# Fused cross-covariance attention and MLP on one core: scores of batch 0 transposed into two PSUM banks, a small first chunk, and v block 2 loaded behind the weights

## The chip, the cores and the metric

One core of one Trainium2 chip runs the whole program. The metric is device time in microseconds (us), lower is better. Most executions of the kernel before agree within 0.3%.

## The reference, cut to what matters

```python
# q, k, v: (4, 6080, 256); moe_w_in: (256, 2048); moe_w_out: (2048, 256)
qn = q / (norm(q, axis=1) + 1e-6);  kn = k / (norm(k, axis=1) + 1e-6)
a  = softmax(kn.transpose(0, 2, 1) @ qn / tau)      # 256 x 256 per batch
x  = (v @ a).reshape(24320, 256)
out = gelu_tanh(x @ w_in) @ w_out
```

Each batch needs all of its q and k before a 256 x 256 matrix is known; then 6080 rows of v stream through it. The kernel folds `a @ w_in` into one matrix `aw` per batch, so that a block of 512 rows costs `hp = v @ aw`, a gelu, and `yp = g @ w_out`.

## The kernel before: the parts that matter here

Batch 0 has nothing to hide behind. Its q and k are loaded in chunks; each is cast (VectorE, DVE), squared (ScalarE, ACT) and multiplied into G (TensorE, PE):

```python
    first_chunks = chunks_of([12, 12, 5, 6, 4, 4, 2, 2], 2)   # slots of 128 rows
    TAIL, SHARED = 4, 6
    fillers = [0, 0, 5, 7, 4, 3, 1, 0]        # idle matmuls that keep the clock up
    ...
    for n, ch in enumerate(first_chunks):
        ...                                    # cast, square
        keep_clock(fillers[n])
        ...                                    # G += k^T q;  cols += column sums of the squares
```

The weights follow the q and k in the load queue. GpSimd (POOL) casts them and, between the casts, issues the loads of v blocks 1 and 2:

```python
    for half in range(2):
        ...                                    # w_in: two loads, two casts
        load_v(1 + half)
    for half in range(2):
        w = flat_stage(8)
        nc.sync.dma_start(out=w, in_=wout_v[:, half * 8 : half * 8 + 8, :])
        nc.gpsimd.tensor_copy(wout_bf[:, half * 8 : half * 8 + 8, :], w)
```

Then the serial end of the head: root of the column sums, scaling of G, four transposes into one tile T, two exponentials, the first columns of `aw`, and the first hp:

```python
    T = turned(Gs)                             # four transposes into one PSUM tile
    keep_clock(1, pY, "y")
    ...
    for jc in range(2):
        nc.scalar.activation(eT[:, jc, :], T[:, jc, :], AF.Exp, scale=r[:, jc : jc + 1])
```

v itself has to be turned. Block 0 and block 1 are turned by TensorE, all later blocks by DMA transposes, which SyncE (SP) issues at the start of the block two before:

```python
        for blk in range(n_blocks):
            vT = vT_of.pop(nb)
            turn_v(nb + 2)                     # four DMA transposes of v block nb + 2
            load_v(nb + 3)                     # GpSimd's queue
            for i in range(NP):                # hp, gelu, and yp of the block before
```

GpSimd's queue also carries batch 1's q and k, from step 3 of block 0 on.

Of the kernel before, what the change touches and what calls it, by code (L numbers as in the profile page):

```python
# [8 lines left out]
FP32 = mybir.dt.float32  # L9
BF16 = mybir.dt.bfloat16  # L10
AF = mybir.ActivationFunctionType
# [7 lines left out]
def kernel(  # L19
# [10 lines left out]
    nc = tc.nc  # L30
# [29 lines left out]
    pA = ctx.enter_context(tc.tile_pool(name="pA", bufs=2, space=bass.MemoryType.PSUM))  # L60
    pH = ctx.enter_context(tc.tile_pool(name="pH", bufs=2, space=bass.MemoryType.PSUM))
    pY = ctx.enter_context(tc.tile_pool(name="pY", bufs=2, space=bass.MemoryType.PSUM))
# [7 lines left out]
    def chunks_of(sizes, with_rem):  # L70
        found, s0 = [], 0
        for n, size in enumerate(sizes):
            found.append((s0, size, n == with_rem))
            s0 += size
        assert s0 == S_ALL
        return found
# [12 lines left out]
    def slots_of(chunk, rest=REM):  # L89
        _, size, rem = chunk  # L90
        return [(s, 128) for s in range(size)] + ([(size, rest)] if rem else [])
# [1 line left out]
    n_all = S_ALL + 1  # L93


    first_chunks = chunks_of([12, 12, 5, 6, 4, 4, 2, 2], 2)
    TAIL, SHARED = 4, 6
    fillers = [0, 0, 5, 7, 4, 3, 1, 0]
    staged = []

    def halves(pool, tag, dtype, size, most=SMAX):

        tiles = [pool.tile([128, 2, most, 256], dtype, tag=tag, name=tag)
                 for _ in range(1 if size <= most else 2)]
        if len(tiles) == 1:
            return [tiles[0][:, x] for x in range(2)], tiles[0]
        return [t.rearrange("p a b c -> p (a b) c") for t in tiles], None
# [21 lines left out]
    ident = const.tile([128, 128], FP32)  # L129
# [20 lines left out]
    def keep_clock(n, pool=pH, tag="h"):  # L150

        for _ in range(n):
            idle = pool.tile([128, 2, 512] if pool is pH else [128, 512], FP32, tag=tag, name="idle")
            nc.tensor.matmul(idle[:, 0, :] if pool is pH else idle, lhsT=filler[:, 0:128], rhs=filler, start=True, stop=True)
# [37 lines left out]
    def turned(Gs):  # L192
        T = pA.tile([128, 2, 256], FP32, tag="a", name="T")
        for ic in range(2):
            for jc in range(2):
                nc.tensor.matmul(T[:, jc, ic * 128 : ic * 128 + 128],  # L196
                                 lhsT=Gs[:, ic, jc * 128 : jc * 128 + 128],
                                 rhs=ident, is_transpose=True)
        return T

    def row_sums(eT):
        rs = pA.tile([128, 512], FP32, tag="a", name="rs")
        for ic in range(2):
            for jc in range(2):
                nc.tensor.matmul(
                    rs[:, ic : ic + 1],
                    lhsT=eT[:, jc, ic * 128 : ic * 128 + 128],
                    rhs=ones_bf,
                    start=jc == 0, stop=jc == 1)
        rsinv = smx.tile([128, 2], FP32, tag="rsinv", name="rsinv")  # L210
        nc.vector.reciprocal(rsinv, rs[:, 0:2])
        return rsinv
# [19 lines left out]
    n_chunks = len(first_chunks)  # L232
    seen, summed = 0, 0

    def sums_of(parts, last):
        nonlocal summed
        for m, x in enumerate(parts):
            col_sums(cols, x, ones_bf[: x[0].shape[0], :], summed == 0, last and m == len(parts) - 1)
            summed += 1
# [16 lines left out]
    for n, ch in enumerate(first_chunks):  # L256
        st, whole = staged[n]
        size = ch[1]
        qkb, qk_whole = halves(qkp, "qk", BF16, size)
        sqb, sq_whole = halves(sqp, "sq", BF16, size)  # L260
        hi = size + ch[2]
        if whole is None:
            todo = list(zip(qkb, sqb, st))
        else:
            todo = [[y[:, :, 0:hi] for y in (qk_whole, sq_whole, whole)]]
        for to, sq, x in todo:
            nc.vector.tensor_copy(to, x)  # L267
            if n != n_chunks - 2:
                nc.scalar.activation(sq, x, AF.Square)  # L269
        if n == n_chunks - 2:  # L270
            nc.scalar.activation(sqb[1][:, 0:hi], st[1][:, 0:hi], AF.Square)
            nc.vector.tensor_mul(sqb[0][:, 0:hi], qkb[0][:, 0:hi], qkb[0][:, 0:hi])
        keep_clock(fillers[n])
        for s, rows in slots_of(ch, 128):
            gram(G, qkb, s, rows, seen == 0, seen == n_all - 1)
            seen += 1
        if waiting is not None:
            pairs_of(*waiting)
            waiting = None
        if n < 2:  # L280
            pairs_of(n, sqb)
        elif n < TAIL:
            waiting = (n, sqb)
        else:
            sums_of([[y[:rows, s, :] for y in sqb] for s, rows in slots_of(ch, 128)], n == n_chunks - 1)

        for x in ((2, 3) if n == 0 else (4, 5) if n == 1 else (n + 4,)):
            stage_chunk(x)

    v0 = stage.tile([128, 2, SMAX, 256], FP32, tag="st", name="v0")  # L290
# [11 lines left out]
    def load_v(nb):  # L302
        if nb >= B * n_blocks:
            return
        r0, n, rest = v_parts(nb)
        t = vin.tile([128, 4, 256], BF16, tag="v", name="vb")
        nc.gpsimd.dma_start(  # L307
            out=t[:, 0:n, :],
            in_=v_rows[r0 : r0 + n * 128, :].rearrange("(p s) c -> p s c", s=n))
        if rest:  # L310
            nc.gpsimd.dma_start(out=t[:rest, n, :], in_=v_rows[r0 + n * 128 : r0 + n * 128 + rest, :])
        v_of[nb] = t
# [36 lines left out]
    for half in range(2):  # L349
        w = flat_stage(2)  # L350
        for x in range(2):
            c0 = half * 1024 + x * 512
            nc.sync.dma_start(out=w[:, :, x * 512 : x * 512 + 512], in_=win_v[:, :, c0 : c0 + 512])
            nc.gpsimd.tensor_copy(win_bf[:, :, c0 : c0 + 512], w[:, :, x * 512 : x * 512 + 512])
        load_v(1 + half)
    for half in range(2):
        w = flat_stage(8)
        nc.sync.dma_start(out=w, in_=wout_v[:, half * 8 : half * 8 + 8, :])
        nc.gpsimd.tensor_copy(wout_bf[:, half * 8 : half * 8 + 8, :], w)  # L359


    r = smx.tile([128, 4], FP32, tag="r", name="r")
# [3 lines left out]
    Gs = scaled(G, r)  # L366
    vps = []
    for cc in range(2):
        p = pH.tile([128, 2, 512], FP32, tag="h", name="vps")[:, 0, :]
        for s in range(4):  # L370
            nc.tensor.matmul(p[:, s * 128 : s * 128 + 128],
                             lhsT=v0[:, s, cc * 128 : cc * 128 + 128],
                             rhs=ident, is_transpose=True)
        vps.append(p)
    keep_clock(1, pY, "y")
    T = turned(Gs)
    keep_clock(1, pY, "y")
    vT0 = vts.tile([128, 2, 512], BF16, tag="vT", name="vT")
    nc.vector.tensor_copy(vT0[:, 0, :], vps[0])
    eT = smx.tile([128, 2, 256], BF16, tag="eT", name="eT")  # L380
    aw = awp.tile([128, 2, D], BF16, tag="aw", name="aw")
    for jc in range(2):
        nc.scalar.activation(eT[:, jc, :], T[:, jc, :], AF.Exp, scale=r[:, jc : jc + 1])  # L383
    nc.scalar.activation(vT0[:, 1, :], vps[1], AF.Copy)


    firsts = []

    def first_aw(n, jc, pool=pY, tag="y"):

        if jc == 0:
            firsts.append(pool.tile([128, 512], FP32, tag=tag, name="ps"))
        nc.tensor.matmul(
            firsts[n][:, 0:256],
            lhsT=eT[:, jc, n % 2 * 128 : n % 2 * 128 + 128],
            rhs=win_bf[:, jc, n // 2 * 256 : n // 2 * 256 + 256],
            start=jc == 0, stop=jc == 1)

    first_aw(0, 0)
    first_aw(1, 0)  # L400
    rsinv = row_sums(eT)
    first_aw(0, 1)
    first_aw(1, 1)
    for n in (2, 3):
        first_aw(n, 0, pA, "a")
        first_aw(n, 1)
    for n in range(4):
        ic, lo = n % 2, n // 2 * 256
        dst, scale = aw[:, ic, lo : lo + 256], rsinv[:, ic : ic + 1]
# [2 lines left out]
        else:  # L412
            nc.vector.tensor_scalar_mul(dst, firsts[n][:, 0:256], scale)  # L413
    nc.scalar.activation(dummy, ones_f, AF.Gelu_apprx_tanh)
    aw_left = [(fs, ic, *((pA, "a") if fs == 2 else (pY, "y"))) for fs in range(1, 4) for ic in range(2)]

    def more_aw(n):
        for _ in range(n):
# [18 lines left out]
    def attention_steps(b, aw_next):  # L437
# [50 lines left out]
        yield  # L488
        T = turned(Gs)
        eT = smx.tile([128, 2, 256], BF16, tag="eT", name="eT")  # L490
        if abs(inv_tau) > TANH_MAX:
            for jc in range(2):
                nc.scalar.activation(eT[:, jc, :], T[:, jc, :], AF.Exp, scale=r[:, jc : jc + 1])
            yield
# [67 lines left out]
    for b in range(B):  # L562
# [5 lines left out]
        for blk in range(n_blocks):  # L568
# [27 lines left out]
            for i in range(NP):  # L596
                at_slot.update(g=g, i=i)
                hp = pH.tile([128, 2, 512], FP32, tag="h", name="hp")
                for j in range(2):
                    fc = 2 * i + j  # L600
                    for cc in range(2):
                        nc.tensor.matmul(hp[:, j, :cols],  # L602
                                         lhsT=aw[:, cc, fc * 128 : fc * 128 + 128],
                                         rhs=vT[:, cc, :cols],
# [4 lines left out]
                if before is not None:  # L609
                    n = -(-len(before["todo"]) // (NP - i))  # L610
                elif i >= NP - 3:

                    n = 4
                else:
                    n = 0
# [14 lines left out]
    for c0 in (0, 128):  # L630
        yp = pY.tile([128, 512], FP32, tag="y", name="yp")[:, 0:128]
        for fc in range(FC):
            nc.tensor.matmul(yp, lhsT=before["g"][:, fc, s * 128 : s * 128 + 128],  # L633
                             rhs=wout_bf[:, fc, c0 : c0 + 128], start=fc == 0, stop=fc == FC - 1)
# [39 lines left out]
```

## Time and profile before

| | value |
|---|---|
| median of 6 runs | 753.86 us (753.45 to 754.20) |
| last k chunk of batch 0 landed | 34.28 us |
| first hp matmul | 40.06 us |
| waits of PE after that | one over 0.25 us: yp on w_out, 0.71 us |
| span of the profiled run | 752.0 us |

The profile is read in three pieces. Up to 34 us loading sets the pace; from there to 40 us a chain of small steps; after 40 us PE, without a gap worth naming. In that last piece any idle microsecond of PE is one of the total. The lines are in the prediction.

### The profile page before, as it was taken

How to read it: one execution, taken by the hardware profiler on the slowest of the kernel's cores; microseconds unless marked ns; L12 is line 12 of the kernel's file. 1: busy time of each engine (PE TensorE's matmuls, PEld its weight loads, DVE VectorE, ACT ScalarE, POOL GpSimd, SP SyncE). 2: the span in 40 equal slices, each digit the busy share in tenths (PEclk: the TensorE clock that was granted, in tenths of full speed). 3: DMA queues.
4: the chain of work that ended last, by engine and by line, in shares of the span. 5: the costliest groups of instructions: out<-in, count | busy, mean ns of one | idle time of the engine just before them, and what ended most of it. 6: DMA issues, size and time to landing. Idle time of an engine off the chain costs nothing.

```text
span 752.0 us, 12341 instructions
## 1 busy us (share of the span) xinstructions
PE 726.4 (97%) x5186; PEld 502.3 (67%) x5274; DVE 284.3 (38%) x497; ACT 420.3 (56%) x411; POOL 80.8 (11%) x154
## 2 busy tenths in 40 slices
PE   2899999999999999999999999999999999999998
PEld 1656766776666766776666666776666666666666
DVE  3733556463501646554521265555351011011011
ACT  4875555556456555555555555555645655555552
POOL 1061111101012102101001102010101000000000
PEclk9999999999999999999999999999999999999999
DMA  9989685613237685824325876671413533322111
GB/s 369 400 205 200 104 150 139 132 43 69 70 72 144 114 163 108 164 63 75 71 57 117 141 119 124 150 143 46 69 43 85 105 85 70 69 75 54 41 57 57
DMA packets 80183, 85.69 MB, mean 114 GB/s; under 512 B 55424, under 2 KB 59136, under 8 KB 79616
## 3 DMA queue, kind: packets, MB, share of 16 engines
q0 software_dynamic: 14480, 30.87, 25.7%
q1 hardware_dynamic: 65344, 52.39, 24.4%
q10 hardware_dynamic: 304, 1.64, 0.5%
q8 instruction: 41, 0.67, 0.4%
q14 instruction: 14, 0.11, 0.0%
HBM read 78.91 MB, written 24.90 MB: 138 GB/s over the span
## 4 chain that ended last, share of the span: by engine, by line
PE 94%; DMA 3%; ACT 1%; issue 1%; DVE 0%; POOL 0%; SPq 0%; DVEq 0%; POOLq 0%
PE yp L528 44%; PE hp L602 43%; PE G L158 4%; PE ps L218 2%; ACT sq L269 1%; DMA st<-in_q_dram 1%; DMA st<-in_k_dram 1%; PE T L196 0%; POOL wout_bf L359 0%; PE yp L633 0%; PE cols L170 0%; DVE qk L267 0%; DVE aw L413 0%; DVE Gs L188 0%; ACT eT L383 0%
## 5 line engine op out<-in xcount | busy, mean ns | idle before, releaser
L606 ACT ACTIVATE g<-hp 128x1024 bf16<-128x1024 f32 (+1 forms) x384 | 389.8, 1015 | 307.0 <-PE hp L602 295.2
L528 PE MATMUL yp<-wout_bf,g 128*128 128x256 bf16 x3024 | 392.0, 273 | 1.6 <-POOL wout_bf L359 0.7
L602 PE MATMUL hp<-vT,aw 128*128 128x512 bf16 (+1 forms) x1456 | 383.9, 377 | 3.8 <-DVE aw L413 0.2
L528 PEld LDWEIGHTS <-g 128*128 128x128 bf16 x3024 | 295.9, 98 | 114.3 <-issue 1.2
L602 PEld LDWEIGHTS <-aw 128*128 128x128 bf16 x1536 | 149.9, 98 | 104.1 <-DVE aw L413 0.5
L545 DVE COPY ysb<-yp 128x512 f32<-128x512 f32 (+1 forms) x95 | 64.9, 683 | 396.5 <-PE yp L528 396.5
L460 DVE TENSOR_TENSOR acc<-acc,sq 128x512 f32<-128x512 f32 x141 | 97.6, 692 | 4.8
L459 DVE TENSOR_TENSOR sq<-qkb 128x512 bf16<-128x512 bf16 x141 | 58.9, 418 | 0.0
L158 PE MATMUL G<-qkb 128*128 128x256 bf16 x288 | 55.0, 273 | 0.0
L307 POOL DMA_DIRECT2D vb<-in_v_dram x47 | 25.9, 552 | 88.6 <-DMA vT<-vb 81.3
L227 DVE TENSOR_SCALAR aw<-ps,rsinv 128x512 bf16<-128x512 f32 x30 | 22.4, 749 | 23.5 <-PE ps L218 18.3
L158 PEld LDWEIGHTS <-qkb 128*128 128x128 bf16 x288 | 28.2, 98 | 3.3
L332 POOL CAST gate<-g 1x1 f32<-1x1 bf16 x24 | 5.9, 245 | 227.8 <-ACT g L606 227.8
L158 PE MATMUL G<-qk 128*128 128x256 bf16 x96 | 13.5, 298 | 15.8 <-DVE qk L267 15.8
L269 ACT ACTIVATE sq<-st 128x3072 bf16<-128x3072 f32 (+2 forms) x9 | 21.1, 2379 | 11.1 <-DMA st<-in_q_dram 8.2
L158 PEld LDWEIGHTS <-qk 128*128 128x128 bf16 x96 | 9.8, 106 | 19.1 <-DVE qk L267 16.6
L267 DVE CAST qk<-st 128x3072 bf16<-128x3072 f32 (+2 forms) x10 | 14.2, 1438 | 13.1 <-DMA st<-in_q_dram 10.0
L218 PE MATMUL ps<-win_bf,eT 128*128 128x512 bf16 x54 | 16.4, 379 | 0.2
L479 POOL TENSOR_TENSOR r<-r,half 128x4 f32<-128x4 f32 x3 | 3.1, 1042 | 103.4 <-DVE r L478 103.4
L82 POOL DMA_DIRECT2D qkb<-in_q_dram x24 | 12.9, 537 | 5.8 <-issue 4.3
L585 POOL COPY g<-gr 128x1024 bf16<-128x1024 bf16 x2 | 2.1, 1036 | 101.3 <-PE yp L528 101.3
L82 POOL DMA_DIRECT2D qkb<-in_k_dram x24 | 12.9, 539 | 0.0
(73 smaller groups left out, 109.0 us busy)
## 6 DMA issues: line engine op xcount, KB each, us to landing
out_dram<-ysb SPq DMA_DIRECT2D x44, 512.0 KB, 3.0
vb<-in_v_dram POOLq DMA_DIRECT2D x43, 256.0 KB, 6.2
qkb<-in_q_dram POOLq DMA_DIRECT2D x21, 384.0 KB, 4.6
qkb<-in_k_dram POOLq DMA_DIRECT2D x21, 384.0 KB, 6.4
st<-in_q_dram SPq DMA_DIRECT2D x2, 1536.0 KB, 11.8
vT<-vb SPq DMA_TRANSPOSE x184, 3.0
wst<-in_moe_w_in_dram SPq DMA_DIRECT2D x4, 512.0 KB, 7.5
wst<-in_moe_w_out_dram SPq DMA_DIRECT2D x2, 1024.0 KB, 11.7
```

The costliest lines, as they stand in the source:

```text
L82: engines[x].dma_start(out=dst[x][:, 0:size, :], in_=src[b, s0 * 128 : (s0 + size) * 128, :].rearrange("(p s) c -> p s c", s=size))
L158: nc.tensor.matmul(G[:, ic, :], lhsT=qk[1][:rows, s, ic * 128 : ic * 128 + 128], rhs=qk[0][:rows, s, :], start=first and ic == 0, stop=las ...
L218: nc.tensor.matmul(ps, lhsT=eT[:, jc, ic * 128 : ic * 128 + 128], rhs=win_bf[:, jc, fs * 512 : fs * 512 + 512], start=jc == 0, stop=jc == 1)
L227: nc.vector.tensor_scalar_mul(dst, ps, scale)
L269: nc.scalar.activation(sq, x, AF.Square)
L307: nc.gpsimd.dma_start(out=t[:, 0:n, :], in_=v_rows[r0 : r0 + n * 128, :].rearrange("(p s) c -> p s c", s=n))
L459: nc.vector.tensor_mul(sq[:rows], flat, flat)
L460: nc.vector.tensor_add(acc[:rows], acc[:rows], sq[:rows])
L528: nc.tensor.matmul(yp[:rows, at, :], lhsT=g[:, fc, s * 128 : s * 128 + rows], rhs=wout_bf[:, fc, :], start=fc == 0, stop=fc == FC - 1)
L545: nc.vector.tensor_copy(ysb[:, s0 : s + 1, :], yp[:, 0 : s + 1 - s0, :])
L602: nc.tensor.matmul(hp[:, j, :cols], lhsT=aw[:, cc, fc * 128 : fc * 128 + 128], rhs=vT[:, cc, :cols], start=cc == 0, stop=cc == 1)
L606: nc.scalar.activation(g[:, 2 * i : 2 * i + 2, :cols], hp[:, :, :cols], AF.Gelu_apprx_tanh)
```

## The change

Its intent: let the first exponential start before all four transposes are done, begin work on a small first chunk, and take v block 2's load out of the way of w_out, for which yp waited.

```diff
-    first_chunks = chunks_of([12, 12, 5, 6, 4, 4, 2, 2], 2)
-    TAIL, SHARED = 4, 6
-    fillers = [0, 0, 5, 7, 4, 3, 1, 0]
+    first_chunks = chunks_of([2, 12, 12, 5, 6, 4, 2, 2, 2], 3)
+    TAIL, SHARED = 4, 7
+    fillers = [0, 0, 0, 5, 7, 4, 1, 1, 0]
 ...
-        load_v(1 + half)
+        if half == 0:
+            load_v(1)
     for half in range(2):
         w = flat_stage(8)
 ...
+    load_v(2)
 ...
-    T = turned(Gs)
-    keep_clock(1, pY, "y")
+    T = [pY.tile([128, 512], FP32, tag="y", name="T") for _ in range(2)]
+    for ic in range(2):
+        for jc in range(2):
+            nc.tensor.matmul(T[jc][:, ic * 128 : ic * 128 + 128], ...)   # cut
 ...
-        nc.scalar.activation(eT[:, jc, :], T[:, jc, :], AF.Exp, scale=r[:, jc : jc + 1])
+        nc.scalar.activation(eT[:, jc, :], T[jc][:, 0:256], AF.Exp, scale=r[:, jc : jc + 1])
```

Cut: the staging of the chunks that goes with the new sizes (the squares of two chunks before the last, where it was one, are split between ACT and DVE), and the PSUM pools of the first products, which swap places, with the row sums moved to a third pool. `TAIL` stays 4, but with one chunk more in front it now leaves the chunk of six among those whose squares are summed slot by slot, 24 column-sum matmuls where pairs took 12.

More of the change, by code (lines that the diff above doesn't have):

```diff
@@ L199, in turned, with row_sums @@
         return T
-    def row_sums(eT):
-        rs = pA.tile([128, 512], FP32, tag="a", name="rs")
+    def row_sums(eT, rs=None):
+        if rs is None:
+            rs = pA.tile([128, 512], FP32, tag="a", name="rs")
         for ic in range(2):
@@ L267 @@
             nc.vector.tensor_copy(to, x)
-            if n != n_chunks - 2:
+            if n not in (n_chunks - 3, n_chunks - 2):
                 nc.scalar.activation(sq, x, AF.Square)
-        if n == n_chunks - 2:
+        if n in (n_chunks - 3, n_chunks - 2):
             nc.scalar.activation(sqb[1][:, 0:hi], st[1][:, 0:hi], AF.Square)
@@ L279 @@
             waiting = None
-        if n < 2:
+        if n < 3:
             pairs_of(n, sqb)
@@ L285 @@
             sums_of([[y[:rows, s, :] for y in sqb] for s, rows in slots_of(ch, 128)], n == n_chunks - 1)
-        for x in ((2, 3) if n == 0 else (4, 5) if n == 1 else (n + 4,)):
+        for x in ((2,) if n == 0 else (3, 4) if n == 1 else (5, 6) if n == 2 else (n + 4,)):
             stage_chunk(x)
@@ L375 @@
     keep_clock(1, pY, "y")
-    T = turned(Gs)
-    keep_clock(1, pY, "y")
+    T = [pY.tile([128, 512], FP32, tag="y", name="T") for _ in range(2)]
+    for ic in range(2):
+        for jc in range(2):
+            nc.tensor.matmul(T[jc][:, ic * 128 : ic * 128 + 128],
+                             lhsT=Gs[:, ic, jc * 128 : jc * 128 + 128],
+                             rhs=ident, is_transpose=True)
     vT0 = vts.tile([128, 2, 512], BF16, tag="vT", name="vT")
@@ L382, with first_aw @@
     for jc in range(2):
-        nc.scalar.activation(eT[:, jc, :], T[:, jc, :], AF.Exp, scale=r[:, jc : jc + 1])
+        nc.scalar.activation(eT[:, jc, :], T[jc][:, 0:256], AF.Exp, scale=r[:, jc : jc + 1])
     nc.scalar.activation(vT0[:, 1, :], vps[1], AF.Copy)
     firsts = []
-    def first_aw(n, jc, pool=pY, tag="y"):
+    def first_aw(n, jc, pool=pA, tag="a"):
         if jc == 0:
@@ L400 @@
     first_aw(1, 0)
-    rsinv = row_sums(eT)
+    rsinv = row_sums(eT, pH.tile([128, 2, 512], FP32, tag="h", name="rs")[:, 0, :])
     first_aw(0, 1)
@@ L404 @@
     for n in (2, 3):
-        first_aw(n, 0, pA, "a")
+        first_aw(n, 0, pY, "y")
         first_aw(n, 1)
@@ L414 @@
     nc.scalar.activation(dummy, ones_f, AF.Gelu_apprx_tanh)
-    aw_left = [(fs, ic, *((pA, "a") if fs == 2 else (pY, "y"))) for fs in range(1, 4) for ic in range(2)]
+    aw_left = [(fs, ic, *((pA, "a") if fs == 1 else (pY, "y") if fs == 2 else (pA, "a"))) for fs in range(1, 4) for ic in range(2)]
     def more_aw(n):
```

## The prediction

> **What bounds the kernel now.** I read the page first, then the chain of waits in order of time for the first 80 us, then the timeline of 0 to 68 us, and last the DMA answers for single issues.
>
> The page's parts 2 and 4:
>
> ```profile
> PE   2899999999999999999999999999999999999998
> PE 94%; DMA 3%; ACT 1%; issue 1%; DVE 0%; POOL 0%; SPq 0%; DVEq 0%; POOLq 0%
> ```
>
> From the third slice on TensorE (PE) is busy to the end. It runs in program order, so a microsecond of idle TensorE removed or added after 40 us is a microsecond of the total. The head before that is a separate stage. Its chain of waits:
>
> ```profile
> 22.02 9.55 DMA st<-in_k_dram
> ...
> 35.98 0.18 ACT r L363
> ...
> 37.30 0.75 PE T L196 x4
> 38.06 0.02 issue
> 38.08 0.48 ACT eT L383
> ...
> 39.52 0.50 DVE aw L413
> 40.01 0.04 issue
> 40.06 1.04 PE hp L602 x4
> ```
>
> The head is loading: DMA is at 9 tenths from the second slice of the head on, and the trace has batch 0's last k chunk landing at 34.28 us. Then comes a serial tail of 5.8 us (square, column sums, root, scaling, transposes, exponential, first product) to the first hp matmul at 40.06. After it, the timeline shows only one idle spell of TensorE worth naming:
>
> ```profile
> 45.96 1.90 POOL L359 CAST wout_bf<-wst 128x2048 bf16<-128x2048 f32 x1 [2.73 <-DMA wst<-in_moe_w_out_dram]
> 48.90 13.50 SPq L321 DMA_TRANSPOSE vT<-vb  x8
> 49.88 1.90 POOL L359 CAST wout_bf<-wst 128x2048 bf16<-128x2048 f32 x1 [2.02 <-PE hp L602]
> 51.83 0.60 PE L528 MATMUL yp<-wout_bf,g 128*128 128x256 bf16 x4 [0.71 <-POOL wout_bf L359]
> ```
>
> The fourth line is the wait that the third part of the change aims at: yp sits 0.71 us until GpSimd has cast the second half of w_out. The third names hp, but the trace has that half landing at 49.83, so the load is what the cast waited for. The second line is where I see the danger: v block 2 and block 3 go through DMA transposes on the SP queue.
>
> **What the Trainium skill says.** "DMA: Bandwidth & Descriptors", section "Queues, rings and completion order": each DMA engine goes round-robin between the queues it has work for, packet by packet, so a queue of small packets beside one of large packets gets its turns but not the bytes. The trace agrees strongly. Time from issue to landing of the transposes (256 B packets), first the one issued alone at 48.90, then the four of v block 3 issued from 57.36, beside the loads that GpSimd issues:
>
> ```profile
> vT<-vb SPq DMA_TRANSPOSE x1, 2.4
> ...
> vT<-vb SPq DMA_TRANSPOSE x4, 9.6
> ```
>
> "TensorE: Matmul & The Clock Gate", Part 1: the array's clock is halved by default and after an idle window of about 3.4 us, and comes back after about as long a busy one. The timeline agrees with the start: 24 G matmuls cold, then 24 warm.
>
> ```profile
> 14.38 4.50 PE L158 MATMUL G<-qk 128*128 128x256 bf16 x24 [14.38 <-DVE qk L267]
> ...
> 20.70 2.79 PE L158 MATMUL G<-qk 128*128 128x256 bf16 x24 [1.24 <-DVE qk L267]
> ```
>
> So a cold restart costs about 4.50 - 2.79 = 1.7 us. "PSUM — Partial Sum Buffer", section "PSUM bank collisions raise a hardware error": two engines must not be in one bank at once, so an exponential that reads T while TensorE still writes T needs T in two banks. In the trace the exponential starts 0.04 us after the fourth transpose's end, as that asks.
>
> **The change part by part.**
>
> *Two banks.* The new loop runs (ic 0, jc 0), (0, 1), (1, 0), (1, 1). The first exponential needs jc 0 of both ic, so it follows three of four transposes, not two. Single records of the trace: the third transpose ends at 37.93, the fourth at 38.04. Gain 0.11 us, and it carries through exponential, row sums, reciprocal and scaling to the first hp. The removed filler matmul (0.38 us) lies in TensorE's wait for the exponential: nothing. The moves between PSUM pools swap two pools of two banks: nothing.
>
> *Small first chunk.* Sizes 12, 12, 5+rest, 6, 4, 4, 2, 2 become 2, 12, 12, 5+rest, 6, 4, 2, 2, 2. Work starts near 5 us in place of 10.90, and buffers come free earlier. But in the trace the loads queue back to back: chunk 2 was issued at 13.69 while chunk 1 landed until 18.28. The bytes (12.45 MB by 34.28 us) don't change. The last chunk is again two slots, squared wholly on ACT (1.06 us) after its landing. ACT and DVE had 0.2 to 1.4 us of idle before each late chunk, so neither was behind. Two-slot chunks land 256 KB in about 0.67 us, four-slot ones 512 KB in about 1.33: no difference. Gain 0 +- 0.15 us.
>
> *v block 2 behind the weights.* Its load was issued at 42.68, landed at 48.88 and shared the engines with w_out. Without it the second half of w_out should land near 48 in place of 49.83 (its packets kept the engines some 1.3 us, an estimate from the packet records of 46 to 49 us). The two casts then run 45.96 to about 49.8, yp wants the result near 51.1, and the 0.71 us idle goes. Gain 0.7 us.
>
> The price: v block 2's load is now issued near 49.8. Alone such a load took 4.7 us (the one issued at 140.84), so it lands near 54.5 in place of 48.88. Its four transposes go out 54.5 to 58.4 in place of 48.90 to 52.81 and now fall wholly among the loads of v 3, batch 1's first two q/k chunks, v 4 and v 5, which in the trace kept the engines from 53 to about 68.7. In that stretch I count 59 to 65 transpose packets per us (65 from 62 to 67), and one block needs 4 x 256 = 1024: 16 us at that rate, or whenever the loads are through. The loads start some 1.5 us earlier and are one v block more, so they are through near 67 to 68; the rest of the transposes then needs under 1 us, and about 1 us to land. So vT 2 is there near 68 (67 to 69.5). The neighbour confirms the size: v block 3's transposes, issued 57.36 to 61.15, landed at 66.79 to 70.12. Block 2's first hp matmul reads vT 2; it started at 64.84 and would now want it at 64.84 - 0.8 = 64.0. In the kernel before vT 2's last piece landed at 61.54, a margin of only 3.3 us. So TensorE stalls about 4.0 us. That is about the length that lets the clock drop; I give it four chances in ten of costing 1.7 us: 0.7.
>
> Sum: -0.1 + 0 - 0.7 + 4.0 + 0.7 = +3.9 us, 757.8.
>
> **The rivals.**
> First, the late load hides anyway: the transposes get more turns than in my count (in 54 to 56 us they did 107 and 124 packets per us; at 110 the 1024 are done near 64.5), and only the gains remain: 753.9 - 0.8 = 753.1. For it: whoever placed the load must have thought it safe, and the rate I use varies twofold. Against it: no block of four transposes that met these loads finished before they did. One chance in four.
> Second, the stall is worse: the loads run slower with the transposes among them from the start, vT 2 lands at 70, and the clock goes cold: 753.9 - 0.8 + 6 + 1.7 = 760.8. One in ten.
> Third, the head becomes faster by a microsecond because the early chunk lets DMA start better. For it: the first 2 us of loading run below the later rate. Against: those are start-up, whatever the chunk. It would make 752.1; one in twelve.
>
> **Range and chances.** With the stall 757.8, without 753.1; weighted by 3 to 1 I put the middle at 757.3. Eight in ten: 752.8 to 760.2. Two per cent is 15 us; no rival reaches it, so within 2% has 0.97.
>
> **What would show it.** Exponential: the first starts after the third transpose, before the fourth ends, and the first hp comes at 39.9 to 40.1. Head: the last k landing within 0.2 us of 34.28. Weights: no wait of yp on wout_bf. Stall: hp waits some 4 us on the transposes near 64 us, shown as idle TensorE, with the granted clock or the next matmuls' durations telling whether it went cold; v block 3's transposes must not stall block 3 as well. I am wrong if vT 2's last transpose lands before 64 us, if w_out's second half still lands near 49.8, or if the last k chunk moves by more than 0.3 us.

## The result, and the profile after

The changed kernel takes 760.95 us (median of 6 runs, 759.30 to 764.88) against 753.86. The ratio is 1.0101, 95% interval 1.0075 to 1.0127. Ratios here are the mean time of one kernel's fast runs over that of the other's of the same rounds, so they are not quite the ratio of the medians quoted. So the kernel is slower by some 7 us (under 1%, but clear of the noise), outside the predicted range of 752.8 to 760.2. Its spread, 5.6 us, is new as well; the kernel before has 0.75.

The profiled run is the slowest of the six (764.88 us, span 763.1). Part 2 of its page, PE's busy share and the granted clock in 40 slices of 19 us:

```profile
PE   3995999999999999999999999999999999999998
...
PEclk9898999999999999999999999999999999999999
```

The fourth slice of PE, 57 to 76 us, is half empty, and the clock was lowered in the second and fourth. PE's timeline there:

```profile
64.89 0.82 PE L535 MATMUL yp<-wout_bf,g 128*128 128x256 bf16 x6
74.25 1.86 PE L609 MATMUL hp<-vT,aw 128*128 128x512 bf16 x4 [8.55 <-DMA vT<-vb]
75.91 1.91 PE L535 MATMUL yp<-wout_bf,g 128*128 128x256 bf16 x8
...
77.88 1.03 PE L609 MATMUL hp<-vT,aw 128*128 128x512 bf16 x4
```

The first hp of block 2 waits 8.55 us for the transposes of v block 2. The restart is cold: from this hp to the next one 3.63 us pass, where a warm round takes 1.95 (77.88 to 79.83), so 1.7 us more are lost. The chain of waits shows where the lateness is made, line by line start, length, what:

```profile
36.33 7.77 DMA wst<-in_moe_w_out_dram
44.10 0.05 issue
44.15 1.89 POOL wout_bf L361
...
48.19 1.80 POOL wout_bf L361
49.99 3.81 DMA vb<-in_v_dram
...
58.20 15.91 DMA vT<-vb
```

It no longer runs through the first hp. It runs from w_out's load through GpSimd's two casts to v block 2's load, landed at 53.81, and its transposes, of which the last took 15.91 us and landed at 74.12. The page's own first hp came at 41.69, 1.63 us later than before, and yp's wait on w_out is gone. The sum closes on the traced pair: 1.63 - 0.71 + 8.55 + 1.7 = 11.2 us, against spans of 763.1 - 752.0 = 11.1.

Two DMA answers of the changed kernel tell how the transposes fared. Queues between 54 and 58 us, while SP was busy issuing the first three (packets, MB, time that the packets took as a share of 16 engines):

```profile
q0 software_dynamic: 335, 0.68, 104.9%
q8 instruction: 1, 0.02, 1.5%
```

SP's queue, q1, isn't in the list: for 4 us after the first issue, at 53.82, not one packet of a transpose went through, while GpSimd's queue q0, filled before, had the engines. Some 1.3 us of that are usual: in the kernel before, the transpose issued alone at 48.90 had nearly all its packets from 50.2 us on. And between 62 and 66 us nearly nothing moved at all:

```profile
DMA packets 73, 0.14 MB, mean 34 GB/s; under 512 B 30, under 2 KB 30, under 8 KB 73
...
q0 software_dynamic: 45, 0.13, 99.7%
```

The engines were not without work there. The 45 packets of q0 took 99.7% of 16 engines' 4 us, some 1.4 us each, where the 335 between 54 and 58 took 0.2 us each. In late_v2_alone, below, the same 4 us moved 0.81 MB at 203 GB/s.

### The profile page after: what moved, and what is told of

Read it like the earlier page. It is cut to its first block, busy times and chain, and to the rows that moved or that the text cites. A ratio compares the mean times of both kernels' runs of the same rounds, so it can differ in the third digit from the quotient of the medians.

```text
span 763.1 us, 12447 instructions
## 1 busy us (share of the span) xinstructions
PE 735.0 (96%) x5279; PEld 503.6 (66%) x5279; DVE 285.0 (37%) x499; ACT 420.1 (55%) x412; POOL 80.1 (10%) x154
## 4 chain that ended last, share of the span: by engine, by line
PE 92%; DMA 6%; SPq 1%; POOL 0%; issue 0%; ACT 0%; DVE 0%; POOLq 0%; ACTq 0%
PE yp L535 42%; PE hp L609 41%; PE G L158 5%; DMA st<-in_k_dram 2%; DMA vT<-vb 2%; PE ps L219 1%; DMA wst<-in_moe_w_out_dram 1%; SPq L322 1%; DMA vb<-in_v_dram 0%; POOL wout_bf L361 0%; PE idle L154 0%; PE cols L170 0%; ACT sq L270 0%; PE yp L640 0%; DVE qk L268 0%
## 5 line engine op out<-in xcount | busy, mean ns | idle before, releaser
L609 PE MATMUL hp<-vT,aw 128*128 128x512 bf16 (+1 forms) x1536 | 391.9, 378 | 8.7 <-DMA vT<-vb 8.5
L158 PE MATMUL G<-qk 128*128 128x256 bf16 x96 | 16.2, 335 | 15.1 <-DVE qk L268 15.1
```

What stands on the lines that cost most here:

```text
L158: nc.tensor.matmul(G[:, ic, :], lhsT=qk[1][:rows, s, ic * 128 : ic * 128 + 128], rhs=qk[0][:rows, s, :], start=first and ic == 0, stop=las ...
L609: nc.tensor.matmul(hp[:, j, :cols], lhsT=aw[:, cc, fc * 128 : fc * 128 + 128], rhs=vT[:, cc, :cols], start=cc == 0, stop=cc == 1)
```

## The experiments

Twelve kernels ran. "First hp" and "PE gap" are from the profiled run: the longest idle time of PE after the first hp, if over 0.25 us.

| run | median us | ratio to before, 95% interval | first hp | PE gap |
|---|---|---|---|---|
| late_v2_alone | 761.00 | 1.0091, 1.0076 to 1.0106 | 40.50 | hp on transposes 4.63 |
| late_v2_late_qk | 754.61 | 1.0008, 0.9992 to 1.0023 | 40.36 | G on q/k 1.22 |
| late_v2_on_pe | 753.84 | 1.0001, 0.9989 to 1.0014 | 40.37 | none |
| v2_between | 756.73 | 1.0032, 1.0011 to 1.0053 | 40.17 | hp on transposes 3.43 |
| no_late_v2 | 753.71 | 0.9995, 0.9981 to 1.0008 | 40.58 | none |
| banks_alone | 753.88 | 1.0004, 0.9990 to 1.0017 | 40.10 | yp on w_out 0.65 |
| chunks_alone | 753.45 | 0.9991, 0.9977 to 1.0004 | 40.61 | none |
| chunks_few_fillers | 753.86 | 1.0000, 0.9986 to 1.0014 | 42.20 | none |
| chunks_warm | 753.92 | 0.9997, 0.9982 to 1.0012 | 40.74 | none |
| chunks_warm_light | 753.76 | 0.9994, 0.9977 to 1.0010 | 40.17 | yp on w_out 0.66 |
| banks_split_wout | 752.86 | 0.9987, 0.9973 to 1.0000 | 39.99 | none |
| split_wout_alone | 752.92 | 0.9985, 0.9973 to 0.9998 | 40.38 | none |

### Which part: late_v2_alone, banks_alone, chunks_alone, no_late_v2

Each part of the change was put alone on the kernel before, and the late load was taken out of the changed kernel.

```diff
 late_v2_alone:  kernel before with
-        load_v(1 + half)
+        if half == 0: load_v(1)      # and load_v(2) after w_out's casts
 banks_alone:    kernel before with T in two pY tiles and the pools swapped
 chunks_alone:   kernel before with the new sizes, fillers and staging
 no_late_v2:     changed kernel with load_v(1 + half)
```

> The kernel before with only v block 2's load moved behind the weights. Theory: the transposes of v block 2 meet the loads of v 3, q/k and v 4 and hold the first hp matmul of block 2; yp's wait on wout_bf (0.71 us) goes, a wait of hp on the transposes of 5 to 9 us near 64 us comes, and a cold restart of about 2 us: 758 to 762 us, and a wider spread than the kernel before. First hp stays at 40.06 +- 0.2. Rival (the stall comes from the head that runs 1.6 us later, or from the pool swap): no wait of hp over 1 us, 753.2.

> The kernel before with only the two banks for the transposed scores and the pool swap. Theory: the first exponential starts 0.11 us earlier, first hp at 39.95, total 753.75. Rival (a pool swap makes a new wait): first hp later than 40.1 or a new wait of PE on a PSUM buffer, 754.2 or more.

> The kernel before with only the new chunk sizes, fillers and staging. Theory: TensorE gets behind in the head (cold at the third chunk of products, then fillers in order), so the first hp comes at 41.7 to 41.9 in place of 40.06 and the rest is as before: 755.4 to 755.8 us. Rival (the later first hp of the whole change comes from the two banks and swapped pools): first hp at 40.1, 753.9.

> The changed kernel with v block 2's load back at its old place (so chunks and banks remain). Theory: 753.3 to 754.0 us, the sum of chunks_alone and banks_alone, whatever the first hp's time between 40.5 and 41.8. Rival (the parts together cost what each alone doesn't): 755.5 or more.

late_v2_alone has the whole loss: 761.00 us, and the changed kernel without it is at 753.71. It also has the spread, 759.72 to 762.47. PE's timeline in its profiled run (759.72 us, the fastest of its four):

```profile
69.15 1.58 PE L604 MATMUL hp<-vT,aw 128*128 128x512 bf16 x4 [4.63 <-DMA vT<-vb]
```

The wait was a little under the 5 to 9 us expected, the cold restart is there (5.58 us for two rounds, where warm ones take 1.95 each). It matters that its first hp came at 40.50 and the changed kernel's at 41.69, and both have the same median: once the transposes are what block 2 waits for, the time runs along w_out, cast, load, transposes, and a head that is late on PE only shortens the wait. The traces fit this. In the kernel before, block 2's first hp started at 64.84; how much later it starts, plus the cold restart, is the whole loss: 4.3 + 1.7 = 6.0 us here (spans 757.9 - 752.0 = 5.9), 9.4 + 1.7 = 11.1 in the changed kernel (11.1).

banks_alone: the chain of waits shows the exponential behind three transposes, as the code says:

```profile
36.82 0.50 DVE Gs L188
37.32 0.04 issue
37.36 0.74 PE T L380 x3
38.10 0.02 issue
38.12 0.48 ACT eT L388
```

From the start of the scaling to the exponential 1.30 us pass (38.12 - 36.82); in the kernel before it was 1.41 (38.08 - 36.67). The 0.11 us are there. But the last k landed at 34.43 in this run and at 34.28 in that of the kernel before, and that scatter is larger: the first hp at 40.10 was not the expected 39.95, and the time shows nothing.

chunks_alone was a miss of mine: I expected 755.4 to 755.8 from a later first hp. The first hp was later by only 0.55 us, and yp's wait on w_out, 0.71 us, was gone, because PE came there later than w_out did. The two cancel.

That the changed kernel's first hp came later still, at 41.69, is not the work of another part: its code up to the scaling is that of chunks_alone and no_late_v2, whose first hp came at 40.61 and 40.58. What differs in the traces is the granted clock: between 19 and 28 us it averaged 0.62 in the changed kernel and 0.81 in the other two, and the 24 G matmuls of the second chunk of twelve took 5.30 us against 4.09 and 4.14. So the first hp of one and the same head code scatters by 1.1 us from trace to trace.

### What the transposes meet: late_v2_late_qk, late_v2_on_pe, v2_between

All three are late_v2_alone with one thing more.

```diff
 late_v2_late_qk:
-            if n in (3, 9):
-                load_qk(b, n // 6)
+            at = (12, 14) if b == 1 else (3, 9)
+            if n in at:
+                load_qk(b, at.index(n))
 late_v2_on_pe:
-            if b == 1 and n == 5:
-                turn_v_on_pe(1)
+            if b == 1 and n in (5, 13):
+                turn_v_on_pe(1 if n == 5 else 2)
-            turn_v(nb + 2)
+            if nb > 0:
+                turn_v(nb + 2)
 v2_between:  load_v(2) between the two casts of w_out, not after them
```

> As late_v2_alone, and batch 1's first two q/k loads moved from steps 3 and 9 to steps 12 and 14 of the first two blocks (about 58 and 61 us in place of 52 and 56). Theory (the transposes lose their turns to the loads that GpSimd issues): the four transposes of v block 2 land within 6 us of their issue, before 64 us, and hp does not wait for them: 753.0 to 754.5 us, unless the later q/k make the first G wait (then up to 2 us on DVE or G). Rival (the load itself is too late, whatever it meets): hp still waits over 3 us near 64 us, 757 us or more.

> As late_v2_alone, but v block 2 is turned by TensorE (8 transposes, in block 1) and not by DMA. Theory (only the DMA transposes of block 2 are late, its load is not): hp doesn't wait near 64 us; 753.86 - 0.7 (yp's wait gone) + 0.45 (8 transposes) = 753.6 us. Rival (the load itself lands too late, near 69 us): a wait of TensorE's transposes on v block 2 near 60 us, 757 or more.

> The kernel before with v block 2's load between the two casts of w_out: issued near 47.9 us, between the old place (42.7) and the late one (50). Theory (the later its transposes go out, the more of them fall among the loads of GpSimd's queue): the load lands at 51 to 53, some of the four transposes still run free, the last lands at 64 to 68 and hp waits 0 to 3.5 us near 64 us: 753.5 to 758. Rival (a fixed cost of any late load): as late_v2_alone, 760 to 762.

With batch 1's q and k out of the way (and v block 5's load, which follows them in GpSimd's queue: issued at 65.03 in place of 57.22), the load of v block 2 is as late as in late_v2_alone (landed at 54.07 against 54.34), yet hp doesn't wait. DMA issues between 48 and 60 us, first late_v2_alone, then late_v2_late_qk: size, median us from issue to landing:

```profile
vT<-vb SPq DMA_TRANSPOSE x4, 10.1
```

```profile
vT<-vb SPq DMA_TRANSPOSE x4, 3.5
```

And its queues between 54 and 58 us, where late_v2_alone has 319 packets of q0 and none of q1:

```profile
q0 software_dynamic: 225, 0.40, 55.9%
q1 hardware_dynamic: 535, 0.12, 49.5%
```

The four transposes were through at 61.09. What was won is partly paid back, as the expectation allowed: the first G of batch 1 now waits for its q and k. PE's waits after 41 us in late_v2_late_qk:

```profile
PE G L158 <- DMA qkb<-in_k_dram: 1.2, 1, 1.2
```

late_v2_on_pe keeps the q and k where they were and takes the transposes of block 2 off the DMA. No wait at all; 753.84 against 753.6 expected. So a load that lands at 54.34 is early enough. Only its DMA transposes, queued beside GpSimd's loads, are not.

v2_between moves the load to 47.48, halfway, and gets part of the cost: 3.43 us in the profiled run, and 754.79 to 758.76 over its four. These fall in two pairs: 758.31 (the traced run) and 758.76 us with a mean granted clock of 0.998, 754.79 and 755.15 with 0.999 and 1.000. The clocks suggest that the latter two had no cold restart; they were not traced. The wait was at the upper end of what was expected, and again cold:

```profile
67.83 1.86 PE L605 MATMUL hp<-vT,aw 128*128 128x512 bf16 x4 [3.43 <-DMA vT<-vb]
```

### The later head: chunks_few_fillers, chunks_warm, chunks_warm_light

All three are chunks_alone with other numbers of idle matmuls:

```diff
-    fillers = [0, 0, 0, 5, 7, 4, 1, 1, 0]      # chunks_alone
+    fillers = [0, 0, 0, 0, 0, 4, 1, 1, 0]      # chunks_few_fillers
+    fillers = [0, 24, 8, 5, 7, 4, 1, 1, 0]     # chunks_warm
+    fillers = [0, 24, 8, 5, 7, 0, 0, 0, 0]     # chunks_warm_light
```

> chunks_alone without the 12 filler matmuls ahead of chunks 3 and 4. Theory (TensorE runs behind from the third chunk on, and the fillers in its order keep it behind): the 24 G matmuls near 21 us still take over 4 us, but the first hp comes at 40.0 to 40.3 us in place of 40.61, yp's wait on wout_bf comes back in part, total 753.4 to 753.9. Rival (the small loads land later, or the last squares wait for something else): first hp stays at 40.6.

> chunks_alone with 24 and 8 more filler matmuls, which fill TensorE's idle time between the small chunk and the first and second chunk of twelve. The run without fillers (chunks_few_fillers) went the wrong way (first hp 42.20), so the theory is now the clock alone. Theory: with the clock kept up the 24 G matmuls near 21 us take 2.79 us and the first hp comes at 40.0 to 40.3 us as in the kernel before, not sooner; total 753.3 to 754.1. Rival (the new chunks delay the end of the head in another way, such as buffers of the squares): first hp stays at 40.6 or later.

> As chunks_warm, without the 6 fillers ahead of the last chunks of 4, 2 and 2. chunks_warm kept the clock up (24 G in 2.79 us) and its first hp still came at 40.74, so the clock alone isn't it. In its trace TensorE works without a pause from 29.7 us, when the chunk of six is cast, to 36.64; 1.4 us of that are those 6 fillers. Theory (TensorE's own queue behind the chunk of six sets the end of the head): the root starts 1.7 to 1.9 us after the last k landing, as in the kernel before (1.70), in place of 2.26, so the first hp comes 5.8 to 6.0 us after that landing, near 40.2; total within 0.3 us of the kernel before. Rival (ACT or DVE is behind, or TensorE goes cold again without them): root 2.2 us or more after the landing.

chunks_few_fillers refuted me: without fillers the first hp came not sooner but at 42.20. In its chain the 12 G matmuls of the chunk of six take 1.88 us where they take 1.31 in chunks_alone, and the 8 after them 1.71 against 0.87: the clock was down. So the fillers seem to be needed; with a scatter of 1.1 us between traces of one head code, one trace of each doesn't settle it, and the time, 753.86 us, shows nothing. chunks_warm then kept the clock up (the 24 G of the second chunk of twelve in 2.79 us, against 4.09 in chunks_alone), and that too didn't bring the first hp back. Its chain showed why:

```profile
29.63 0.05 issue
29.68 1.49 PE G L158 x12
31.16 0.98 PE cols L170 x40
32.14 0.89 PE idle L154 x4
33.03 0.87 PE G L158 x8
...
36.66 0.18 ACT r L363
```

From the cast of the chunk of six to the root, every piece is PE, 7 us without a pause. The new order puts that chunk two slots later in the load stream and leaves PE, behind it, its own work, 24 column sums and 6 fillers. In the kernel before PE still waited for a cast in that stretch (0.16 us, at 32.95). chunks_warm_light takes the 6 fillers out, and PE is ahead again. Its timeline, and then its chain:

```profile
35.26 0.61 PE L158 MATMUL G<-qk 128*128 128x256 bf16 x4 [0.40 <-DVE qk L267]
```

```profile
36.09 0.18 ACT r L363
```

The root follows the last landing (34.42) by 1.67 us; 1.70 in the kernel before, 2.26 in chunks_warm. So with these fillers the new chunks are as good as the old. And as the first hp moved back to 40.17, yp's wait on w_out came back, 0.66 us: w_out is ready at a time of its own, near 51.8 us, and PE that comes sooner waits for it.

### A version that beats both: banks_split_wout, split_wout_alone

yp's wait can be removed where it arises. The second half of w_out is loaded and cast in two pieces, so that yp goes on with the first:

```diff
-        nc.sync.dma_start(out=w, in_=wout_v[:, half * 8 : half * 8 + 8, :])
-        nc.gpsimd.tensor_copy(wout_bf[:, half * 8 : half * 8 + 8, :], w)
+        for lo, hi in ((0, 8),) if half == 0 else ((0, 3), (3, 8)):
+            nc.sync.dma_start(out=w[:, lo:hi, :], in_=wout_v[:, half * 8 + lo : half * 8 + hi, :])
+            nc.gpsimd.tensor_copy(wout_bf[:, half * 8 + lo : half * 8 + hi, :], w[:, lo:hi, :])
```

> Two banks, old chunks, v block 2 loaded where it was; w_out's second half loaded and cast in two pieces (3 and 5 of its 8 column groups), so that yp can go on with the first. Theory: yp's wait of 0.71 us goes without any late transpose: 753.1 us, and no wait of PE over 0.3 us after the first hp. Rival: the smaller cast comes no earlier because it waits for the same landing near 49.8 us, then 753.9.

> The kernel before with only w_out's second half loaded and cast in two pieces, banks left out. Theory: the 0.7 us of yp's wait are gained, and the two banks are worth 0.1 us on top: 753.1 us here, against 752.86 of banks_split_wout. Rival (the banks carry the gain): 753.8.

GpSimd's timeline in banks_split_wout; the first line holds the casts of the first half and of the first piece:

```profile
45.56 2.66 POOL L361 CAST wout_bf<-wst 128x2048 bf16<-128x2048 f32 x2 [2.30 <-DMA wst<-in_moe_w_out_dram]
...
50.01 1.25 POOL L361 CAST wout_bf<-wst 128x1280 bf16<-128x1280 f32 x1 [1.78 <-DMA wst<-in_moe_w_out_dram]
```

PE has no gap over 0.25 us after its first hp. 752.86 and 752.92 us, 0.13 and 0.15% under the kernel before; the interval of the first touches 1.0000, that of the second doesn't. The two don't differ, so the banks' 0.1 us is not seen in the time here either.

## Why the prediction was wrong

The direction was right, the danger was named, and the range missed by 0.75 us at the median.

**Two banks, -0.11.** Right: 1.41 us became 1.30. Hidden in the total by landings of the last k that scatter by some 0.4 us from run to run.

**Small first chunk, 0 +- 0.15.** Right for the total (chunks_alone 0.9991, an interval with 1 in it) and for its grounds: the last k landed within 0.05 us of before. Wrong on the way there: I had looked at ACT and DVE for slack before the late chunks, and not at PE, which fell behind, by 0.5 us in chunks_alone and, with the clock lowered for longer, 1.6 in the changed kernel. The total doesn't show it, because yp's wait absorbs up to 0.7 us.

**Weights, -0.7.** Right: the wait is gone, the second half landed at 48.10 (near 48 was predicted).

**Late transposes, +4.0: the term that was mis-sized.** The load landed at 53.81 (54.5 predicted), the wait came where it was said, and its cause is shown: late_v2_late_qk and late_v2_on_pe leave the load late and have no wait. The step that failed is "they are through near 67 to 68": in the changed kernel's trace the last of those loads landed at 73.84, the last transpose at 74.12, and hp waited 8.55 us. In late_v2_alone they landed at 68.31 and 69.01, the second inside my 67 to 69.5, and hp waited 4.63. I had taken a rate of 59 to 65 transpose packets per us as holding from the start. In fact none went through for the first 4 us, in both traces; and in the changed kernel's there are 4 us more, 62 to 66, in which all queues together moved 34 GB/s, with packets of 1.4 us. Why that stretch arises, and in which of the untraced runs, stays open. Such delays varying between runs would fit the spread of 759.3 to 764.9 us, which I had not foreseen at all; that is argued, not shown.

**Cold restart, +0.7.** Mis-sized too: I gave it four chances in ten. All three traced kernels with a wait of 3.4 us or more paid 1.6 to 1.7 us. The mean clocks of the untraced runs agree: 0.991 to 0.996 in the changed kernel's six, 0.997 or 0.998 in the four of no_late_v2, which has the same head and no wait. So all six seem to have paid. The size of 1.7 was right, the chance far too low.

With the wait of late_v2_alone's trace and a certain restart my own sum would have been -0.8 + 4.6 + 1.7 = +5.5, or 759.4, near the fastest runs of the changed kernel. The median run can be worked back in the same way, as an estimate: 760.95 - 753.86 = 7.1 us, less 1.7 for the restart, puts block 2's first hp 5.4 us after 64.84, at 70.2, where I had 68. So of the 3.2 us by which the median missed 757.8, some 2.2 are later transposes and 1.0 the restart that I had discounted.

**The rivals.** The first, that the late load is hidden, had one chance in four, and no run of the changed kernel or of late_v2_alone supports it. The second, a worse stall and a cold clock at 760.8 us, is what came in size; I gave it one in ten. Its reason, loads slowed by the transposes among them from the start, is not what the traces show: for the first 4 us there was no transpose among them. So that its number fits is in part luck. The middle was drawn down by the first rival, and not as stated: 757.8 and 753.1 weighted 3 to 1 give 756.6, not 757.3. The third, a faster head, didn't come.

## What to carry to other kernels

Before a load is moved out of the way of something urgent, follow its data to the last consumer and ask what traffic the steps behind it will then meet: here a wait of 0.7 us was traded for four transposes of which two had run free (2.4 and 2.3 us from issue to landing, the other two 6.1 and 8.7) and which now all had to queue behind bulk loads. A latency measured alone (2.4 us) or even a rate measured in traffic says little about a transfer that starts when other queues are already full; take the neighbours that did meet that traffic, and their worst. And where a wait is for the last piece of a large transfer, cut the piece before moving anything else.

## What the Trainium skill lacked or had wrong

- "DMA: Bandwidth & Descriptors", section "Queues, rings and completion order", says that an engine takes its queues in turn, packet by packet. The changed kernel's trace shows that a transpose issued behind a full queue did not get its first turn soon: issued at 53.82, no packet of SP's queue between 54 and 58 us, while GpSimd's queue sent 335 (late_v2_alone: none against 319). Alone, issued at 48.90 in the kernel before, most of its packets came from 50.2 us on. The page has nothing on how long a DMA transpose may wait for its first packet behind other queues.
- None of the pages that I read has the stretch of 62 to 66 us in the changed kernel's trace, in which 73 packets moved in 4 us at 34 GB/s, those of GpSimd's queue at some 1.4 us each. It belongs to the same page.
- Nothing was found wrong in "TensorE: Matmul & The Clock Gate", Part 1, by which an idle window of about 3.4 us brings the lower clock back: waits of 3.43, 4.63 and 8.55 us were all followed by a cold restart that cost 1.6 to 1.7 us.
